# A two-layer attention and MLP stack on one core: start order of the first four tiles, narrow masks, and turns ahead of queries

## The chip, the cores and the metric

The kernel runs on one core of a Trainium2 chip. The metric is device time in microseconds of one execution. The engines are TensorE (PE for matmuls, PEld for its weight loads), VectorE (DVE), ScalarE (ACT), GpSimd (POOL) and SyncE (SP), which issues the DMAs. Each engine runs its own instructions in the order in which they were laid down and waits on semaphores for the others.

## What is computed

Four blocks one after the other on x of shape (1, 2048, 576) in bf16: linear attention A, MLP B, then A and B again with the same weights. Each has a layer norm in front and a residual sum behind.

```python
def _A_ref(x, wqkv, wo):
    B, S, D = x.shape
    H = 32; Dh = D // H
    qkv = (lambda x, *d: x.transpose(*d))((x @ wqkv).reshape(B, S, 3, H, Dh), 2, 0, 3, 1, 4)
    q, k, v = qkv[0], qkv[1], qkv[2]
    phi = lambda t: jnp.where(t > 0, t + 1, jnp.exp(t)) + 1e-6
    pq, pk = phi(q), phi(k)
    kv = jnp.einsum("bhsd,bhse->bhde", pk, v)
    z = jnp.einsum("bhsd->bhd", pk)
    num = jnp.einsum("bhqd,bhde->bhqe", pq, kv)
    den = jnp.einsum("bhqd,bhd->bhq", pq, z)[..., None] + 1e-6
    o = num / den
    return (lambda x, *d: x.transpose(*d))(o, 0, 2, 1, 3).reshape(B, S, D) @ wo

def _B_ref(x, w1, b1, w2, b2):
    y = _layernorm(x, axis=-1)
    h = _gelu(jnp.einsum("bsd,df->bsf", y, w1) + b1)
    return jnp.einsum("bsf,fd->bsd", h, w2) + b2

x = x + _A_ref(_layernorm(x, axis=-1), A_wqkv, A_wo)
x = x + _B_ref(_layernorm(x, axis=-1), B_w1, B_b1, B_w2, B_b2)
x = x + _A_ref(_layernorm(x, axis=-1), A_wqkv, A_wo)
x = x + _B_ref(_layernorm(x, axis=-1), B_w1, B_b1, B_w2, B_b2)
```

## The kernel before

The 2048 rows are 16 tiles of 128. The 576 columns are five blocks of 128 (the last half empty) when they are contracted, and five groups of heads (126, 126, 126, 126 and 72 columns) for the queries. The MLP works on chunks of 512 rows. All matmul operands are bf16; sums are in PSUM, of which four banks form the pool `ps_h` (each holds one product of keys, queries or turned columns until ScalarE or VectorE has read it), and two pairs are accumulators.

The change lies in the first attention layer (`li == 0` in `layer_A`). Its first sweep goes over the tiles t. A tile is loaded from x (`load_x0`), normalised, turned, and then used twice.

*Normalising* is a small pipeline, `LNPipe`. `feed0(t)` puts tile t into it, and each `lnp.tick()` moves every tile one stage on: statistics on VectorE (L363, L364, L370, named s..a, s..b and g.. for the first tiles, and L381, named u..), the reciprocal root (ScalarE's Ln and Exp for tiles 0 and 1, L394 and L396; GpSimd's pow for the others, L399), then the scaling. For tiles 0 to 3 VectorE scales 512 columns (L416, n..) and GpSimd the last 64 into `v_ring` (L414); from tile 4 on GpSimd does both (L402, L410). The last stage is the *turn*: five TensorE transposes into PSUM (`tp`, L464) and copies into `yT` (L466 by ScalarE and L467 by VectorE for tiles 0 to 3, named ca.. and cd..; L469 by ScalarE alone from tile 4 on). A tick with `transposes=0` turns no tile.

*Keys* (`keys(t)`, two `k_half`, L601): ten matmuls of yT with the key weights into two banks. The feature map phi follows in one of two ways: `phi_from_psum` has two ScalarE passes (L511 exp, L512 identity) and two short VectorE instructions on bf16 (L517, L519); `phi_by_dve` has one ScalarE pass (L494) and two VectorE instructions (L496, and L498, which reads the bank). The second half of each tile goes by VectorE, and in tiles 2, 6, 10 and 14 the first half too.

*Queries* (`q_proj(g, c)`, L578): five matmuls for a group of heads g and a chunk c of 512 rows, then phi in the first way. There are twenty; `q_left` holds those still to do, and each takes its place between other work. For g = 0 a memset (L583) writes rows of ones beside the result.

*Sums over rows* (`rows_by_keys(t, half)`, L626): five matmuls of the tile with phi of its keys, added over all tiles. The first sweep does the first half of the columns, a second sweep the second half.

Behind the first sweep the accumulators are copied out (L638, L641), and in the second sweep `kv_groups((0, 1))` (L650) multiplies by the value weights and cuts the heads' blocks out with the mask `maskz` (L656). The denominators use `head_sel` (L742), `quad_mask` (L785) and `head_bc` (L798, L814). These four masks are constants, built on GpSimd by memsets (L70) and affine selects (L66). `masks(n)` issues the next n steps of the list: one per turn for t = 5 to 12, then two per tile in the second sweep; a scheduling edge puts each behind the last normalisation known at that point, and none waits for more.

What sets the order: TensorE's instructions of this layer are chained in program order (`pe`). On VectorE and ScalarE a scheduler places the instructions, and for the first tiles two lists written by hand, `in_order("...")`, fix the sequence by name. In these names e, id, mi and ma are the four steps of phi (L511 or L494, L512, L517 or L496, L519 or L498), followed by tile and half. In a turn t from 4 on the program has keys(t), then `pre_a1(t)` (which feeds tile t + 3, ticks, and issues a piece of weight load on SP), a query, another tick, and the row sums.

Of the kernel before, what the change touches and what calls it, by code (L numbers as in the profile page):

```python
# [8 lines left out]
ALU = mybir.AluOpType  # L9
# [25 lines left out]
def build(tc, A_x, A_wqkv, A_wo, B_w1, B_b1, B_w2, B_b2, out, dbg=None, n_layers=4):  # L35
    nc = tc.nc
    dbg = dbg or {}
    with ExitStack() as ctx:
# [32 lines left out]

        def inner_diag(tile_, lead, n):
            return [fill(tile_, 1.0),
                    select(tile_[:], 0.0, ALU.is_ge, 0, lead(1) + [[-DH, n]] + ([[0, DH]] if tile_ is maskz else []), 1),
                    select(tile_[:], 0.0, ALU.is_ge, DH - 1,
                           lead(-1) + [[DH, n]] + ([[0, DH]] if tile_ is maskz else []), -1)]

        hb = head_bc[:, :, 0:126].rearrange("p g (h d) -> p g h d", h=7)
        mask_steps = inner_diag(maskz, lambda sign: [], 7) + [
            lambda: nc.gpsimd.memset(zsel[96:P, 0, :], 1e-6),  # L80
        ] + inner_diag(head_sel, lambda sign: [[126 * sign, G]], H) + [
            fill(quad_mask, 1.0),
            select(quad_mask[:], 0.0, ALU.is_ge, 0, [[-32, 4], [0, P]], 1),
            select(quad_mask[:], 0.0, ALU.is_ge, 31, [[32, 4], [0, P]], -1),
            fill(head_bc, 0.0),
        ] + [select(hb, 1.0, ALU.not_equal, -32 * quad, [[-7, G], [-1, 7], [0, DH]], 1) for quad in range(4)]

# [225 lines left out]
        class LNPipe:  # L313
# [11 lines left out]
            def tick(self, transposes=1):  # L325
                land()
                for it in list(self.items):
# [77 lines left out]
                    elif st in (2, 3) and it["kind"] == "A" and it["evac"] == "act":  # L405
                        xt, t = it["xt"], it["t"]
                        tail = first_tail(t)[:, 0:64]
                        if it["norm"] == "pool":
                            for out, cols in ((xt[:, 0:4 * P], slice(0, 4 * P)), (tail, slice(4 * P, D))):
                                norm = nc.gpsimd.tensor_scalar(out=out, in0=xt[:, cols], scalar1=it["rstd"][:, 0:1],  # L410
                                                               scalar2=it["nmr"][:, 0:1], op0=ALU.mult, op1=ALU.add)
                            pool_last["norm"] = norm.ins.name
                        else:
                            nc.gpsimd.tensor_scalar(out=tail, in0=xt[:, 4 * P:D], scalar1=it["mv"][:, 0:1],  # L414
                                                    scalar2=it["rstd"][:, 0:1], op0=ALU.subtract, op1=ALU.mult)
                            norm = nc.vector.tensor_scalar(out=xt[:, 0:4 * P], in0=xt[:, 0:4 * P], scalar1=it["mv"][:, 0:1],  # L416
                                                           scalar2=it["rstd"][:, 0:1], op0=ALU.subtract, op1=ALU.mult)
                            dve_last["norm"] = named(f"n{t}", norm).ins.name
                        row_of[t] = xt
# [152 lines left out]
        def layer_A(li, next_kind, pre_a1=None):  # L572
            pq = {}

            def q_proj(g, c, defer=False):
# [6 lines left out]
                if g == 0:  # L582
                    nc.gpsimd.memset(pq[(g, c)][96:P, 0:CA], 1.0)  # L583
                phi = lambda after=None, dve_after=None, exp_first=False: phi_from_psum(qp[0:GR[g], :], pq[(g, c)][0:GR[g], 0:CA], GR[g], CA,
# [13 lines left out]
            def k_half(t, half, defer=False):  # L598
                kp = ps_h.tile([P, 512], F32, name="k_ps", tag="h")
                for k in range(KD):  # L600
                    pe(nc.tensor.matmul(kp[:, 0:HALF], lhsT=yT[:, k, t * P:(t + 1) * P],  # L601
                                        rhs=wqkv_sb[:, k, D + half * HALF: D + (half + 1) * HALF],
                                        start=(k == 0), stop=(k == KD - 1)))
                by_dve = half or li == 0 and t % 4 == 2

# [69 lines left out]
            if li == 0:  # L675
# [4 lines left out]
                def feed_and_tick(t, n):  # L680
                    feed0(t, after=dve_last["phi"] if t > 5 else None)
                    for _ in range(n):
                        lnp.tick()

                k_half(0, 0)
                phi = k_half(0, 1, defer=True)
                keys(1)
                feed_and_tick(3, 2)
                rows_by_keys(0, 0, (0, 1, 2, 3))
                keys(2)  # L690
                phi()
                feed_and_tick(4, 2)
                rows_by_keys(1, 0, (0, 1, 2, 3))
                rows_by_keys(2, 0, (0, 1, 2, 3))
                keys(3)
                q_proj(*q_left.pop(0))
                feed_and_tick(5, 1)
                feed_and_tick(6, 2)
                in_order("s0a s0b s1b g0 s1a g1 n0 n1 cd0 s2a s2b cd1 g2 u2 mi00 s3a ma00 n2 s3b mi10 cd2 g3 mi11 u3 ma11 "
                         "s4b n3 mi20 ma10 ma20 s4a cd3 g4 u4 mi21 mi01 ma21 ma01 s5a s5b mi30 g5 ma30 u5 mi31 ma31")  # L700
                in_order("ln0 re0 ln1 re1 ca0 ca1 e00 id00 e10 e11 ca2 id10 e20 e21 e01 ca3 e30 e31 id30 ca4")
                rows_by_keys(3, 0, (0, 1, 2, 3))
                for t in range(4):
                    rows_by_keys(t, 0, (4,))
                for t in range(4, NT):
                    keys(t)
                    pre_a1(t)
                    if 4 < t < 13:
                        masks(1)
                    q_proj(*q_left.pop(0), defer=True)(after=act_last["turned"])  # L710
                    lnp.tick()
                    rows_by_keys(t, 0)
                for _ in range(2):
                    q_proj(*q_left.pop(0))
            LAG = 3
            steps = [(t, 1) for t in range(NT)] if li == 0 else [(t, half) for half in range(2) for t in range(NT)]
            behind = []
            for n, (t, half) in enumerate(steps):
                if li == 0:
                    masks(2)  # L720
                    rows_by_keys(t, 1)
                    if t == 3:
                        q_proj(*q_left.pop(0))
                else:
# [315 lines left out]
        lnp.tick()  # L1040
        warm_pe(1)
        lnp.tick()

# [77 lines left out]
```

## Time and profile before

| What | Value |
|---|---|
| Runs shown | 767.79, 767.87, 769.43 us; median 767.87 |
| The profiled execution | 769.74 us, of which the span is 767.9 us |
| TensorE matmuls (PE) busy | 757.9 us, 99% of the span, 6538 instructions |
| VectorE, ScalarE, GpSimd busy | 272.5, 326.2 and 129.5 us |
| Chain that ended last | 96% PE, 2% DVE, 1% DMA, 1% ACT |
| Mean granted clock of TensorE | 0.998 |
| First attention layer | 0 to 110 us, the first MLP starts at 110 |

The chain that ended last follows the work back from the end: where it names TensorE, nothing but TensorE's own work stood in the way; where it names another engine, TensorE waited for that engine. A table of waits gives, for each waiting line, the engine and line that ended the wait. The granted clock is the share of TensorE's full speed in a stretch.

By stage, first sweep (columns: stretch in us, its length, then busy time and count of PE, PEld, DVE, ACT, POOL, then clock, share of the DMA engines, GB/s):

```profile
7.60:22.40 14.80, 12.88 (x100) 9.04 (x100) 13.16 (x51) 8.99 (x22) 9.72 (x18) 1.00 1.01 299
29.50:32.80 3.30, 3.30 (x27) 2.38 (x26) 2.77 (x9) 2.73 (x8) 2.32 (x5) 1.00 1.10 287
52.90:59.90 7.00, 4.95 (x26) 3.11 (x25) 4.59 (x8) 2.99 (x7) 5.83 (x8) 0.76 1.00 169
```

### The profile page before, as it was taken

The page shows a single profiled execution, that of the slowest core. Times are in us where ns is not written, and L with a number is a line of the kernel's source. Part 1 is how long each engine was busy: PE and PEld are TensorE (multiplying, and loading weights), DVE is VectorE, ACT ScalarE, POOL GpSimd, SP SyncE. Part 2 cuts the span into 40 slices and gives each one's busy share as a digit, 9 for nine tenths or more (in the row PEclk, how much of TensorE's full clock was granted, in tenths as well). Part 3 has the DMA queues.
Part 4 walks back from the last instruction along what each step waited for, and adds up shares of the span by engine and source line. Part 5 has one row for each costly group of instructions (what it writes and reads, how often), then busy time and mean ns, then how long its engine had stood idle before and what let it go on. Part 6 is the DMA issues. An engine that isn't in the chain of part 4 may idle for free.

```text
span 767.9 us, 15683 instructions
## 1 busy us (share of the span) xinstructions
PE 757.9 (99%) x6538; PEld 489.7 (64%) x6538; DVE 272.5 (35%) x675; ACT 326.2 (42%) x726; POOL 129.5 (17%) x203
## 2 busy tenths in 40 slices
PE   8989999999999999999999999999999999999998
PEld 5667664575477447645777767447745764674476
DVE  8883865035213603400355668610140032000000
ACT  5764766403620560165046568560065027205600
POOL 6781132012100201110110005200020021001000
PEclk9999999999999999999999999999999999999999
DMA  8992373115502631230147007630141033011000
GB/s 254 262 310 48 106 263 99 50 47 144 158 17 64 186 82 40 93 90 1 47 128 233 3 1 220 245 81 13 49 111 52 16 124 82 9 32 55 2 9 24
DMA packets 80897, 73.82 MB, mean 96 GB/s; under 512 B 36730, under 2 KB 65466, under 8 KB 80826
## 3 DMA queue, kind: packets, MB, share of 16 engines
q1 hardware_dynamic: 80826, 72.82, 32.3%
q8 instruction: 51, 0.84, 0.5%
q14 instruction: 20, 0.16, 0.1%
HBM read 48.03 MB, written 24.77 MB: 95 GB/s over the span
## 4 chain that ended last, share of the span: by engine, by line
PE 96%; DVE 2%; DMA 1%; ACT 1%; POOL 0%; issue 0%; SPq 0%; DVEq 0%; POOLq 0%
PE m_ps L1011 36%; PE h_ps L953 20%; PE hp_ps L953 16%; PE q_ps L578 6%; PE wo_ps L834 5%; PE k_ps L601 5%; PE k_ps L626 4%; PE m_half L1011 1%; PE k_tail L626 1%; PE tp L464 1%; DMA wqkv_sb<-in_A_wqkv_dram 1%; PE rden_ps L798 0%; PE kv_ps L650 0%; PE den_ps L771 0%; DVE pq L824 0%
## 5 line engine op out<-in xcount | busy, mean ns | idle before, releaser
L1011 PE MATMUL m_ps<-w_sb,hT 128*128 128x288 bf16 x2232 | 274.8, 286 | 0.0
L1011 PEld LDWEIGHTS <-hT 128*128 128x128 bf16 x2304 | 224.8, 98 | 59.8 <-issue 3.4
L953 PEld LDWEIGHTS <-w_sb 64*128 64x128 bf16 x2304 | 124.5, 94 | 136.4 <-issue 1.9
L953 PE MATMUL hp_ps<-yT,w_sb 64*128 64x512 bf16 x1152 | 178.0, 376 | 0.0
L953 PE MATMUL h_ps<-yT,w_sb 64*128 64x512 bf16 x1152 | 147.9, 376 | 0.0
L958 ACT COPY relay_sb<-relay_sb 128x1 f32<-128x1 f32 x144 | 28.5, 198 | 260.7 <-PE h_ps L953 217.7
L949 ACT ACTIVATE hT<-h_ps,b1T 128x512 bf16<-128x512 f32 x144 | 91.0, 683 | 43.9 <-PE h_ps L953 43.9
L399 POOL TENSOR_TENSOR ln_rstd<-ln_u,neg_half 128x1 f32<-128x1 f32 x62 | 35.9, 581 | 414.1 <-DVE ln_u L381 220.0
L949 ACT ACTIVATE hT<-hp_ps,b1T 128x512 bf16<-128x512 f32 x144 | 91.1, 692 | 0.0
L562 DVE TENSOR_TENSOR xbf<-m_ps,xo 128x576 bf16<-128x576 f32 x15 | 11.4, 758 | 212.3 <-PE m_ps L1011 212.3
L562 DVE TENSOR_TENSOR xo<-m_ps,xo 128x576 f32<-128x576 f32 x16 | 12.1, 758 | 175.6 <-PE m_ps L1011 175.6
L545 POOL TENSOR_TENSOR xo<-xo,b_bc 128x576 f32<-128x576 f32 x32 | 40.9, 1282 | 98.6 <-DMA xo<-x_d 61.0
L953 PE MATMUL h_ps<-yT,w_tail 64*128 64x512 bf16 x144 | 54.1, 376 | 0.0
L953 PE MATMUL hp_ps<-yT,w_tail 64*128 64x512 bf16 x144 | 54.1, 376 | 0.0
L578 PE MATMUL q_ps<-yT,wqkv_sb 128*126 128x512 bf16 (+1 forms) x200 | 50.7, 385 | 2.8 <-DVE pk L498 2.8
L601 PE MATMUL k_ps<-wqkv_sb,yT 128*128 128x288 bf16 x320 | 46.8, 286 | 1.8 <-DVE ln_u L381 0.9
L834 PE MATMUL wo_ps<-kvwo,pq 126*128 126x288 bf16 (+1 forms) x320 | 44.2, 286 | 0.1
L953 PEld LDWEIGHTS <-w_tail 64*128 64x128 bf16 x288 | 27.1, 94 | 17.1
L601 PEld LDWEIGHTS <-yT 128*128 128x128 bf16 x320 | 31.1, 98 | 10.6 <-ACT yT L469 1.2
L834 PEld LDWEIGHTS <-pq 126*128 126x128 bf16 (+1 forms) x320 | 29.8, 97 | 10.0 <-DVE pq L824 0.5
L578 PEld LDWEIGHTS <-wqkv_sb 128*126 128x126 bf16 (+1 forms) x200 | 25.8, 133 | 15.1 <-issue 3.6
L511 ACT ACTIVATE phi_e<-q_ps 126x512 bf16<-126x512 f32 (+1 forms) x40 | 23.9, 598 | 20.2 <-PE q_ps L578 20.2
(132 smaller groups left out, 611.8 us busy)
## 6 DMA issues: line engine op xcount, KB each, us to landing
xo<-x_d SPq DMA_DIRECT2D x48, 288.0 KB
x_d<-xo SPq DMA_DIRECT2D x32, 288.0 KB
xl<-x_d SPq DMA_DIRECT2D x24, 288.0 KB
y_d<-turned SPq DMA_DIRECT2D x40, 144.0 KB
w_sb<-in_B_w_dram SPq DMA_DIRECT2D x6, 864.0 KB
yT<-y_d SPq DMA_DIRECT2D x10, 512.0 KB
w_sb<-in_B_w_dram SPq DMA_DIRECT2D x9, 512.0 KB
x_d<-xn SPq DMA_DIRECT2D x16, 288.0 KB
```

The costliest lines, as they stand in the source:

```text
L399: nc.gpsimd.tensor_tensor(out=rstd[:], in0=it["u"][:], in1=neg_half[:], op=ALU.pow)
L511: exp = nc.scalar.activation(out=e_out, in_=ps_ap, func=ACT.Exp)
L545: nc.gpsimd.tensor_tensor(out=xo[:], in0=xo[:], in1=b2_bc[:], op=ALU.add)
L562: total = nc.vector.tensor_tensor(out=xn[:, cols].rearrange("p (h n) -> p h n", h=2), in0=halves, in1=xo[:, cols].rearrange("p (h n) -> p ...
L578: pe(nc.tensor.matmul(qp[0:GR[g], :], lhsT=wqkv_sb[:, k, GO[g]:GO[g] + GR[g]], rhs=yT[:, k, c * CA:(c + 1) * CA], start=(k == 0), stop=(k ...
L601: pe(nc.tensor.matmul(kp[:, 0:HALF], lhsT=yT[:, k, t * P:(t + 1) * P], rhs=wqkv_sb[:, k, D + half * HALF: D + (half + 1) * HALF], start=(k ...
L626: pe(nc.tensor.matmul(dst, lhsT=lhsT, rhs=pk, start=(t == 0), stop=(t == NT - 1)))
L834: pe(nc.tensor.matmul(wp[:, half, 0:HALF], lhsT=pq[(g, c)][0:GR[g], j * P:(j + 1) * P], rhs=kvwo[g][0:GR[g], half * HALF:(half + 1) * HALF ...
L949: act_last["gelu"] = nc.scalar.activation(out=to, in_=ps, func=ACT.Gelu_apprx_tanh, bias=b1T[:, f:f + 1], scale=1.0).ins.name
L953: mm = pe(nc.tensor.matmul(dst[n], lhsT=wt, rhs=mv, start=(seen[n] == 0), stop=(seen[n] == 8)))
L958: relay = nc.scalar.copy(out=relay_sb[:, 1:2], in_=relay_sb[:, 0:1])
L1011: pe(nc.tensor.matmul(acc[half][:, 0:HALF], lhsT=hT[f][:, j * P:(j + 1) * P], rhs=w2_sb[:, f, half * HALF:(half + 1) * HALF], start=(f == ...
```

## The change

Masks: three of the four masks (`maskz`, `quad_mask`, `head_bc`) are first made narrow on GpSimd, one column per head or quarter in a shared tile `narrow`, and VectorE copies them out to their width in the second sweep (`wide_masks`, t = 0, 1, 2). `head_sel` and a row of `zsel` are made as before. The list now has 15 steps, and `masks(2)` runs in every turn from t = 4.

First tiles: the 64-column tail of tiles 0 to 3 is scaled by VectorE (nt..) instead of GpSimd; the ones rows of the queries are set by VectorE in this layer; only tile 2 has both halves of its keys by VectorE. The keys of tile 0's first half stand ahead of the turn of tile 1, a second warm-up matmul stands in front, two queries are done before t = 4 instead of one, and both `in_order` lists are new. One query less is done in the second sweep (at t = 3).

Turns: in turn 4 a tick stands ahead of the query, and the tick behind the query turns no tile.

```diff
-        def inner_diag(tile_, lead, n):
-            return [fill(tile_, 1.0),
-                    select(tile_[:], 0.0, ALU.is_ge, 0, lead(1) + [[-DH, n]] + ([[0, DH]] if tile_ is maskz else []), 1),
-                    select(tile_[:], 0.0, ALU.is_ge, DH - 1,
-                           lead(-1) + [[DH, n]] + ([[0, DH]] if tile_ is maskz else []), -1)]
-
-        hb = head_bc[:, :, 0:126].rearrange("p g (h d) -> p g h d", h=7)
-        mask_steps = inner_diag(maskz, lambda sign: [], 7) + [
+        narrow = {}
+
+        def narrow_tile():
+            narrow["all"] = blk.tile([P, D], BF16, name="narrow", tag="blk")
+            return nc.gpsimd.memset(narrow["all"][:, 0:64], 1.0)
+
+        def cut(start, shape, fill, op, base, pattern, mult):
+
+            def step():
+                n = shape[0] * shape[-1] if len(shape) > 1 else shape[0]
+                part = narrow["all"][:, start:start + n]
+                if len(shape) > 1:
+                    part = part.rearrange("p (a b) -> p a b", a=shape[0])
+                return nc.gpsimd.affine_select(out=part, in_=part, compare_op=op, fill=fill, base=base, pattern=pattern,
+                                               channel_multiplier=mult)
+            return step
+
+        lead = lambda sign: [[126 * sign, G]]
+        mask_steps = [
+            narrow_tile,
+            cut(0, (7,), 0.0, ALU.is_ge, 0, [[-DH, 7]], 1),
+            cut(0, (7,), 0.0, ALU.is_ge, DH - 1, [[DH, 7]], -1),
+            cut(8, (4,), 0.0, ALU.is_ge, 0, [[-32, 4]], 1),
+            cut(8, (4,), 0.0, ALU.is_ge, 31, [[32, 4]], -1),
+            lambda: nc.gpsimd.memset(narrow["all"][:, 12:47], 0.0),
+        ] + [cut(12, (G, 7), 1.0, ALU.not_equal, -32 * quad, [[-7, G], [-1, 7]], 1) for quad in range(4)] + [
+            fill(head_sel, 1.0),
...
             lambda: nc.gpsimd.memset(zsel[96:P, 0, :], 1e-6),
-        ] + inner_diag(head_sel, lambda sign: [[126 * sign, G]], H) + [
-            fill(quad_mask, 1.0),
-            select(quad_mask[:], 0.0, ALU.is_ge, 0, [[-32, 4], [0, P]], 1),
-            select(quad_mask[:], 0.0, ALU.is_ge, 31, [[32, 4], [0, P]], -1),
-            fill(head_bc, 0.0),
-        ] + [select(hb, 1.0, ALU.not_equal, -32 * quad, [[-7, G], [-1, 7], [0, DH]], 1) for quad in range(4)]
+            lambda: nc.gpsimd.memset(head_bc[:, :, 126:P], 0.0),
+        ]
+
+        def wide_masks(i):
+            small = narrow["all"]
+            if i == 0:
+                wide = nc.vector.tensor_copy(out=maskz[:], in_=small[:, 0:7].unsqueeze(2).to_broadcast([P, 7, DH]))
+            elif i == 1:
+                wide = nc.vector.tensor_copy(out=quad_mask[:], in_=small[:, 8:12].unsqueeze(2).to_broadcast([P, 4, P]))
+            else:
+                wide = nc.vector.tensor_copy(out=head_bc[:, :, 0:126].rearrange("p g (h d) -> p g h d", h=7),
+                                             in_=small[:, 12:47].rearrange("p (g h) -> p g h", g=G).unsqueeze(3)
+                                             .to_broadcast([P, G, 7, DH]))
+            tc.add_manual_dep(wide.ins, dve_last["phi"], NOSYNC, reason="masks are not urgent")
...
-                            nc.gpsimd.tensor_scalar(out=tail, in0=xt[:, 4 * P:D], scalar1=it["mv"][:, 0:1],
-                                                    scalar2=it["rstd"][:, 0:1], op0=ALU.subtract, op1=ALU.mult)
-                            norm = nc.vector.tensor_scalar(out=xt[:, 0:4 * P], in0=xt[:, 0:4 * P], scalar1=it["mv"][:, 0:1],
-                                                           scalar2=it["rstd"][:, 0:1], op0=ALU.subtract, op1=ALU.mult)
-                            dve_last["norm"] = named(f"n{t}", norm).ins.name
+                            for name, out, cols in ((f"n{t}", xt[:, 0:4 * P], slice(0, 4 * P)), (f"nt{t}", tail, slice(4 * P, D))):
+                                norm = named(name, nc.vector.tensor_scalar(
+                                    out=out, in0=xt[:, cols], scalar1=it["mv"][:, 0:1], scalar2=it["rstd"][:, 0:1],
+                                    op0=ALU.subtract, op1=ALU.mult))
+                            dve_last["norm"] = norm.ins.name
...
-                    nc.gpsimd.memset(pq[(g, c)][96:P, 0:CA], 1.0)
+                    (nc.gpsimd if li > 0 else nc.vector).memset(pq[(g, c)][96:P, 0:CA], 1.0)
...
-                by_dve = half or li == 0 and t % 4 == 2
+                by_dve = half or li == 0 and t == 2
...
                 k_half(0, 0)
+                lnp.tick()
                 phi = k_half(0, 1, defer=True)
                 keys(1)
+                phi()
                 feed_and_tick(3, 2)
                 rows_by_keys(0, 0, (0, 1, 2, 3))
                 keys(2)
-                phi()
                 feed_and_tick(4, 2)
                 rows_by_keys(1, 0, (0, 1, 2, 3))
                 rows_by_keys(2, 0, (0, 1, 2, 3))
                 keys(3)
                 q_proj(*q_left.pop(0))
+                phi = q_proj(*q_left.pop(0), defer=True)
                 feed_and_tick(5, 1)
                 feed_and_tick(6, 2)
-                in_order("s0a s0b s1b g0 s1a g1 n0 n1 cd0 s2a s2b cd1 g2 u2 mi00 s3a ma00 n2 s3b mi10 cd2 g3 mi11 u3 ma11 "
-                         "s4b n3 mi20 ma10 ma20 s4a cd3 g4 u4 mi21 mi01 ma21 ma01 s5a s5b mi30 g5 ma30 u5 mi31 ma31")
-                in_order("ln0 re0 ln1 re1 ca0 ca1 e00 id00 e10 e11 ca2 id10 e20 e21 e01 ca3 e30 e31 id30 ca4")
+                phi(after=first_ones["ca4"].ins.name)
+                in_order("s0a s0b g0 s1a s1b n0 nt0 g1 cd0 n1 nt1 s2a s2b g2 cd1 u2 mi00 s3a s3b n2 nt2 g3 ma00 u3 s4a cd2 "
+                         "mi11 mi10 n3 nt3 ma11 ma10 mi20 ma20 cd3 s4b mi01 g4 u4 ma01 s5a s5b mi30 mi21 ma30 g5 ma21 u5 "
+                         "mi31 ma31")
+                in_order("ln0 re0 ln1 re1 ca0 e00 ca1 id00 e10 e11 ca2 e01 id10 e20 e21 ca3 e30 id30 e31 ca4")
                 rows_by_keys(3, 0, (0, 1, 2, 3))
...
                     pre_a1(t)
-                    if 4 < t < 13:
-                        masks(1)
+                    if t == 4:
+                        lnp.tick()
+                    masks(2)
                     q_proj(*q_left.pop(0), defer=True)(after=act_last["turned"])
-                    lnp.tick()
+                    lnp.tick(transposes=0)
                     rows_by_keys(t, 0)
                 for _ in range(2):
                     q_proj(*q_left.pop(0))
+                masks(len(mask_steps))
...
                 if li == 0:
-                    masks(2)
+                    if t in (0, 1, 2):
+                        wide_masks(t)
                     rows_by_keys(t, 1)
-                    if t == 3:
-                        q_proj(*q_left.pop(0))
...
-        warm_pe(1)
-        lnp.tick()
+        warm_pe(2)
```

## The prediction

> **What bounds the kernel now.** The page comes first: TensorE is busy 99% of the span of 767.9 us and has 96% of the chain that ended last, so time is won only where TensorE stands still or runs slowly, or where the chain leaves it. The page's clock row shows only nines, because one of its slices covers 19.2 us. I therefore read TensorE's waits over the first 110 us, which contain the whole first attention layer:
>
> ```profile
> PE q_ps L578 <- DVE pk L498: 2.8, 3, 2.1
> PE warm_ps L185 <- DVE y_ring L180: 1.3, 1, 1.3
> PE k_ps L601 <- DVE ln_u L381: 0.9, 1, 0.9
> PE k_ps L601 <- DMA wqkv_sb<-in_A_wqkv_dram: 0.5, 1, 0.5
> PE tp L464 <- POOL x L410: 0.4, 1, 0.4
> PE k_ps L601 <- ACT phi_a L512: 0.4, 1, 0.4
> ```
>
> The columns after the colon are total us, times, longest. Everything idle is in the stage that the diff touches, and 2.1 us of it is one wait. The chain of waits around it:
>
> ```profile
> 51.13 1.16 PE q_ps L578 x5
> 52.30 0.02 issue
> 52.32 0.60 ACT phi_e L511
> 52.92 0.02 issue
> 52.95 1.29 DVE phi_e L517
> ...
> 54.35 0.63 DVE pq L519
> 54.98 0.94 DVE phi_e L496
> 55.92 0.02 issue
> 55.94 0.47 DVE pk L498
> 56.41 0.04 issue
> 56.45 2.29 PE q_ps L578 x5
> 58.74 0.24 PE k_tail L626
> 58.98 0.96 PE k_ps L626 x4
> 59.94 1.26 PE k_ps L601 x10
> ```
>
> The chain leaves TensorE for ScalarE and VectorE, and when it comes back the same five query matmuls take 2.29 us instead of 1.16. The timeline shows who held VectorE, and the table by stage shows why the matmuls were slow (columns: us, then busy time and count of PE, PEld, DVE, ACT, POOL, then granted clock, DMA share, GB/s):
>
> ```profile
> 54.66 4.27 POOL L66 TENSOR_SCALAR_AFFINE_SELECT head_bc<-head_bc 128x630 bf16<-128x630 bf16 x4
> 54.91 1.00 DVE L496 TENSOR_SCALAR phi_e<-phi_e 128x288 bf16<-128x288 bf16 x1
> ```
>
> ```profile
> 55.00:56.00 1.00, 0.00 (x0) 0.00 (x0) 0.96 (x2) 0.15 (x1) 0.93 (x2) 1.00 1.16 279
> 57.00:58.00 1.00, 1.00 (x4) 0.51 (x3) 0.44 (x1) 0.00 (x0) 0.93 (x2) 0.50 1.38 21
> ```
>
> The L496 form takes 0.23 us in quiet tiles and 1.00 here. The wide selects of 1.016 us start at 54.66, so the second ends near 56.7 and the first near 55.67; L496 ends at 55.91, which is 55.67 plus its usual 0.23. VectorE's bf16 tensor_scalar waited out a whole GpSimd instruction. After 2.05 us without a matmul the clock was 0.50 until about 59.5.
>
> **The hole (masks).** Key tiles in quiet turns start 3.27 us apart (L601 at 29.42, 32.69, 35.95, 39.22). From 52.73 to 59.74 it took 7.01, and the next ten key matmuls 1.47 instead of 1.39. The hole is worth 3.74 + 0.08 = 3.82 us, of which 2.05 is idle and some 1.77 the half clock. The change removes its cause: the wide GpSimd steps are 0.21 + 2 x 0.334 (maskz), 0.52 + 2 x 0.664 (quad_mask), 0.64 + 4 x 1.016 (head_bc), 7.43 us. In their place stand ten narrow steps (7 to 64 columns). No row has such a form; the bounds are 0.10 (memset 128x1) and 0.35 us (select 128x160), and I take 0.20, near the 0.21 of the 36-column copy L222, so 2.0 us in all, two to four steps per turn. GpSimd works some 2.3 us of each 3.3 us turn, and a turned tile is ready 1.1 us ahead (x and tail of tile 14 end at 49.60, its turn starts at 50.69), which hides them. Uncovered, 0.7 us per turn would show. The steps end by t = 11, long before the masks' first use (kv_ps, 70.4). Gain 3.82, with 2.05 as the low end if the clock fell for another reason.
>
> **Spreading.** Three VectorE copies of 126 + 512 + 630 elements. Bounds: 0.65 us at the pace of tensor_scalar (512 in 0.24 to 0.29), 1.67 at that of the f32 sums (576 in 0.758); they read with a repeat, so I take 1.67. They stand behind the last query's phi and ahead of kvT. VectorE has 5.2 of 10 us free between 60 and 70, and in the new order it is through some 1.5 us ahead of the kv_ps product. Cost 0; uncovered 1.67 at most.
>
> **Keys of tiles 6, 10, 14.** Before, both halves of these tiles went over VectorE's L496/L498, which free the PSUM bank late: the turns from 25.70 to 29.42 and 39.22 to 42.94 took 3.72 us instead of 3.27. Only tile 2 keeps this. ScalarE gets one pass more (L512, 0.31 to the next start), exactly what it does in the quiet turns, where it still waits 0.43 us for each query. Gain 2 x 0.45 = 0.90; the third lies in the hole.
>
> **Ones rows of the queries.** Four memsets of 32x512 move from GpSimd (0.56 each, one of which held tile 4's normalisation from 15.23 to 15.75) to VectorE. By the row of 128x320 in 0.33 us it is 0.53, bounds 0.33 and 0.78 (64x864). VectorE has some 0.3 us free per turn (2.94 us from one L363 to the next in the turn at 32.26, of 3.27), and a product of keys is ready 0.6 to 0.75 us before TensorE wants it; I cost it at 0, uncovered 3 x 0.53 in the loop.
>
> **The start.** I went through the new order by hand with the durations above, keeping the DMA times. Tile 0 is ready 0.24 us earlier because s1 no longer stands ahead of g0, and its 64-column tail comes from VectorE (bounds 0.15, ln_u, and 0.41, 128x512; I take 0.17) instead of GpSimd (0.71). None of it counts: the second half of the key weights lands at 7.63, as before. From there: keys of tiles 0 and 1 until 9.7; tile 2's copies end at 10.83, so its keys start at 10.87 (before 10.88); tile 3 is turned at 12.2 instead of 12.29, keys 3 start at 13.84 instead of 13.77, because product 2 waits for ma20 behind the later e20. The first query is at 15.1, and now the second follows at once at 16.25, while GpSimd finishes tile 4 at 16.75 (before 17.09: u4 is 0.3 later, the memset of 0.53 is gone). TensorE is at tile 4's turn at 17.4, not held; the 0.44 is gone. Keys 4 at 18.66, tile 5's turn at 19.9 (ready at 19.35), its copy done at 21.1 behind the third query, keys 5 at 21.97 without the 0.87. Before it was 22.42, with one query less. That query is taken out of the later loop, where it cost 1.08 (67.50). From t = 5 on the old order already had the turn ahead of the query, so nothing more comes from that. Gain 0.45 + 1.08 = 1.53. Bounds: if all VectorE additions (4 x 0.17 + 0.53 = 1.2) fall on the path, 0.3; if the 0.41 before keys 2 also closes, 1.95.
>
> **Sum.** 3.82 + 0.90 + 1.53 = 6.25 us. The profiled execution is 769.74 us for a span of 767.9, so 1.84 lie around the span; with the change 763.5 in the same measure. The median of the runs is 767.87, 1.87 below that execution, and I carry the difference over: 761.6. The later stages move forward as they are: SP's order is unchanged, the weight loads end near 60 us either way, and w_sb is first needed at 110.
>
> **Rivals.**
> 1. VectorE bounds the start: it has 13.2 of 14.8 us busy between 7.6 and 22.4, and gets five instructions more, 1.2 us. Against: it stands still for 1.6 us there, and my pass found place for them. Start gain 0.3, so 767.87 - 5.02 = 762.9.
> 2. The clock did not fall because of the gap, and the 1.77 stays: 763.4. For it speaks only that the other gaps, up to 0.87 us, left the clock at 1.00, so no row gives a threshold; against it, that it fell at the end of the longest gap. The Trainium skill ("TensorE: Matmul & The Clock Gate", What's actually happening) puts the fall after an idle window of about 3.4 us. By that rule a gap of 2.05 us would not do, and the sum would be 4.5; the trace (0.50 right behind 2.05 us) speaks otherwise.
> 3. The stall moves: GpSimd's extra steps make each tile late at its turn, which now stands ahead of the query at every t. At 0.3 us in 11 turns, 3.3 us: 764.9. Against: the 1.1 us in hand.
> 4. Slower: the half clock comes at the start. In the new hand-written order s4a, which needs tile 4's row from DRAM, stands near 9.95 and ahead of tile 2's copy; before, it stood at 12.92. If the row landed only then (the latest that the trace allows, as s4a did not wait), the keys of tile 2 would wait some 2.3 us, longer than the 2.05 that halved the clock before. Each us of TensorE work done at 0.50 costs one us more, so it decides against the change from 6.25 us of such work less the wait itself, some 4; if all 12.9 us of work between 7.6 and 22.4 ran so, the time would be 767.87 - 6.25 + 12.9 = 774.5. Against: the gap at 54.4 cost only 1.77 in this way, and summed over half microseconds the DMA rates put tile 4's row at about 8.5.
> 5. All of it cancels within 0.2%: some 767.9.
>
> **How the numbers follow.** Forecast 0.62; rival 1 0.13, rival 2 0.06, rival 3 0.09, rival 4 0.06, rival 5 0.04. The predicted time is the forecast's. About 0.2% (1.5 us) is what a measurement of this kernel can tell from no change. Faster: 0.62 + 0.13 + 0.06 + 0.09 = 0.90; same 0.04; slower 0.06. The range's low end takes the better start and 0.5 us for small waits in the two loops, 760.7; its high end takes rival 3 and the bound of the ones rows at one place, 765.4. Above lie rivals 4 and 5, below little.
>
> **What would show it.** Turns of 3.27 us from t = 5 to 15 with clock 1.00 throughout, no wait of q_ps for pk L498, no GpSimd instruction above 0.85 us between 22 and 60, keys 5 near 22.0, and the second sweep starting near 59.8 instead of 64.9. Wrong would be a granted clock below 1 after 6 us, waits of tp for GpSimd's x, DVE copies of the masks ending after kv_ps, or k_ps waiting for copies between 10 and 14 us by more than 0.4.

## The result and the profile after

| What | Before | After |
|---|---|---|
| Median of the runs measured together | 768.21 us (4 runs, 767.79 to 769.43) | 763.48 us (4 runs, 763.10 to 763.75) |
| Ratio, 95% interval | | 0.9935 [0.9918, 0.9953] |
| A second measurement on another occasion | 768.27 us (15 runs) | 763.32 us (5 runs), 0.9932 [0.9918, 0.9945] |
| The profiled execution, its span | 769.74, 767.9 us | 763.75, 762.0 us |
| GpSimd busy | 129.5 us | 119.9 us |

The change makes the kernel faster by some 4.8 us. The forecast was 761.6 us within 760.7 to 765.4; the time lies inside, 1.9 us above the forecast. Profiled execution against profiled execution the step is 5.9 us of span where 6.25 were forecast, so the 1.9 is not a gain that failed to come: it is mostly a matter of what was compared with what, as the runs below show.

TensorE's waits over the first 110 us after the change (engine, line and tile that waited, the engine and line waited for, then total us, times, longest):

```profile
PE warm_ps L214 <- DVE y_ring L209: 1.3, 1, 1.3
PE k_ps L630 <- DVE yT L496: 0.4, 1, 0.4
PE k_ps L655 <- DVE pk L527: 0.3, 1, 0.3
```

The three waits of queries for VectorE's pk (2.8 us), the 0.9 before keys 5, the 0.5 for the key weights' DMA, the 0.4 for GpSimd's x and the 0.4 for phi_a are gone; what is left sits ahead of 14 us. The three stretches shown for the kernel before, or their counterparts (stretch, length, busy time and count of PE, PEld, DVE, ACT, POOL, then clock, DMA share, GB/s):

```profile
52.90:59.90 7.00, 7.00 (x47) 4.86 (x45) 4.58 (x15) 5.76 (x15) 0.00 (x0) 1.00 1.02 178
22.20:57.80 35.60, 35.60 (x272) 26.58 (x270) 29.90 (x104) 28.99 (x66) 23.26 (x53) 1.00 1.01 286
7.60:22.40 14.80, 14.09 (x113) 10.16 (x112) 13.41 (x52) 10.02 (x25) 7.15 (x14) 1.00 1.01 296
```

Between 52.90 and 59.90 GpSimd does nothing now, TensorE is busy for all 7.00 us (4.95 before) and the clock is 1.00 (0.76 before). In the whole first sweep from tile 5 on TensorE has no gap. VectorE's share of the start rose by only 0.25 us (13.16 to 13.41), GpSimd's fell by 2.57.

What the new instructions cost, from the groups of GpSimd over the first 64 us (count, busy us, mean ns) and from VectorE's timeline (start, duration):

```profile
L85 POOL TENSOR_SCALAR_AFFINE_SELECT narrow<-narrow 128x35 bf16<-128x35 bf16 x4 | 1.1, 284 | 0.1
L85 POOL TENSOR_SCALAR_AFFINE_SELECT narrow<-narrow 128x4 bf16<-128x4 bf16 x2 | 0.5, 264 | 0.0
L76 POOL MEMSET narrow<- 128x64 bf16 x1 | 0.2, 153 | 0.0
```

```profile
62.20 0.28 DVE L108 CAST maskz<-narrow 128x126 f32<-128x126 bf16 x1
62.40 0.42 DVE L110 COPY quad_mask<-narrow 128x512 bf16<-128x512 bf16 x1
62.73 0.80 DVE L112 COPY head_bc<-narrow 128x630 bf16<-128x630 bf16 x1
65.04 0.42 DVE L685 TENSOR_TENSOR kvT<-kv_ps,maskz 126x252 bf16<-126x252 f32 x1 [1.51 <-PE kv_ps L679]
```

The narrow steps are 4 to 64 columns wide (the prediction said 7 to 64) and take 0.12 to 0.28 us where 0.20 was put down, 2.3 us in all instead of 2.0. The three spreading copies take 1.50 us together (1.67 was put down), and VectorE then stands still for 1.51 us until TensorE's kv_ps: they are hidden.

### The profile page after: what moved, and what is told of

It reads as the page before. It is cut to its first block, busy times and chain, and to the rows that moved or that the text cites. A ratio compares the mean times of both kernels' runs of the same rounds, so it can differ in the third digit from the quotient of the medians.

```text
span 762.0 us, 15698 instructions
## 1 busy us (share of the span) xinstructions
PE 756.5 (99%) x6539; PEld 489.6 (64%) x6539; DVE 271.0 (36%) x686; ACT 326.6 (43%) x729; POOL 119.9 (16%) x195
## 4 chain that ended last, share of the span: by engine, by line
PE 97%; DVE 2%; ACT 0%; issue 0%; ACTq 0%; DVEq 0%
PE m_ps L1045 36%; PE h_ps L987 20%; PE hp_ps L987 16%; PE q_ps L607 6%; PE k_ps L630 5%; PE wo_ps L868 4%; PE k_ps L655 4%; PE m_half L1045 1%; PE k_tail L655 1%; PE tp L493 1%; PE warm_ps L214 1%; PE rden_ps L832 0%; PE kv_ps L679 0%; DVE xn L591 0%; DVE pq L858 0%
## 5 line engine op out<-in xcount | busy, mean ns | idle before, releaser
L1045 PEld LDWEIGHTS <-hT 128*128 128x128 bf16 x2304 | 224.8, 98 | 59.8 <-issue 3.4
L540 ACT ACTIVATE phi_e<-k_ps 128x288 bf16<-128x288 f32 x31 | 12.8, 412 | 41.5 <-PE k_ps L630 39.3
```

What stands on the lines that cost most here:

```text
L540: exp = nc.scalar.activation(out=e_out, in_=ps_ap, func=ACT.Exp)
L1045: pe(nc.tensor.matmul(acc[half][:, 0:HALF], lhsT=hT[f][:, j * P:(j + 1) * P], rhs=w2_sb[:, f, half * HALF:(half + 1) * HALF], start=(f == ...
```

## The experiments

The edits below are against the kernel before or the changed one, as each says. Starts of keys in TensorE's timeline (us) are the common scale, because from tile 5 on a quiet turn takes 3.27 us everywhere:

| Kernel | keys 5 | keys 14 | keys 15 | span | median of runs |
|---|---|---|---|---|---|
| before, first profile | 22.42 | 52.73 | 59.74 | 767.9 | 768.21 |
| before, e5 | 22.10 | 52.40 | 59.43 | 767.5 | 769.37 (one) |
| before, e6 | 22.24 | 52.54 | 57.96 | 766.0 | 767.91 (one) |
| e1 masks alone | 22.44 | 52.99 | 56.71 | 764.6 | 766.55 |
| e2 keys alone | 22.38 | 51.76 | 56.70 | 764.6 | 766.51 |
| e3 start alone | 21.81 | 52.50 | 56.50 | 764.0 | 766.00 |
| e7 masks and keys | 22.48 | 51.88 | 55.14 | 763.1 | 764.91 |
| e4 changed, old masks | 22.20 | 51.63 | 54.90 | 764.7 | 764.71 |
| after, first profile | 22.20 | 51.64 | 54.90 | 762.0 | 763.48 |
| after, e11 | 21.91 | 51.35 | 54.61 | 761.6 | 763.32 |
| e12 start reordered | 22.79 | 52.23 | 55.49 | 762.4 | 764.28 |

### One part alone: e1, e2, e3

e1 takes the new list of masks, `wide_masks` and the two calls of `masks`, and leaves the rest of the kernel before:

```diff
-                    if 4 < t < 13:
-                        masks(1)
+                    masks(2)
...
-                    masks(2)
+                    if t in (0, 1, 2):
+                        wide_masks(t)
                     rows_by_keys(t, 1)
```

> The kernel before with only the masks made narrow on GpSimd and spread by VectorE. Theory (wide selects hold VectorE, the gap halves the clock): the hole of 3.82 us closes, but tile 14's keys still go over VectorE alone, 0.45, so 3.37 us less, about 764.5 us by the median before of 767.9; granted clock 1.00 from 52 to 60 us. Rival (the half clock has another cause than the gap): only the idle part goes, 1.6 us less, 766.3, and the clock still falls near 56 us. Rival (the spreading copies are not hidden): 1.5 us of the gain come back between 60 and 70 us, 766.0.

Measured: 766.55 us, 0.9974 [0.9964, 0.9985]. The clock is 1.00 throughout and no wide select holds VectorE any more. Tile 14's turn takes 3.72 us, exactly the 0.45 too long that its keys cost. From the first profile to this one the span fell by 3.3 us (767.9 to 764.6), as the theory had it. Yet the median fell by only 1.3 us against the 767.9 of the expectation, and by 2.1 against the 768.62 measured beside it. The spreading was not to blame, since no wait stands between 60 and 72 us. Tile 10's turn took 3.97 instead of 3.72. The trace shows where VectorE fell behind, one turn earlier:

```profile
37.34 0.42 DVE L548 TENSOR_TENSOR pq<-phi_a,phi_e 126x512 bf16<-126x512 bf16 x1 [0.79 <-POOL pq L612]
```

It waits 0.79 us for GpSimd's memset of the ones rows (0.43 before), because `masks(2)` now puts a select of `head_sel` (0.36 us) ahead of that memset, and VectorE's steps behind it start 0.38 later. In the changed kernel VectorE sets these rows itself, so it does not wait for GpSimd there.

e2 shares the first-half keys of tiles 6, 10 and 14 between ScalarE and VectorE, and leaves the wide masks:

```diff
-                by_dve = half or li == 0 and t % 4 == 2
+                by_dve = half or li == 0 and t == 2
```

> The kernel before with only the first-half keys of tiles 6, 10 and 14 given to both ScalarE and VectorE. Theory: the turns of tiles 6 and 10 take 3.27 instead of 3.72 us, tile 14's 0.45 lies in the hole that stays, so 0.9 us less, 767.0. Rival (ScalarE's extra pass delays the queries by as much): nothing, 767.9. Rival (the hole is set by tile 14's late bank, not by the selects): about 4.2 us less, 763.7.

Measured: 766.51 us, 0.9970 [0.9959, 0.9980]. The two turns are 3.27 as expected, so the 0.9 is there; but the hole shrank as well. TensorE's timeline of this run (start, duration, in brackets the wait ahead of it and who ended it), and the clock in the same place:

```profile
53.34 1.24 PE L578 MATMUL q_ps<-yT,wqkv_sb 128*126 128x512 bf16 x5
56.09 0.28 PE L626 MATMUL k_tail<-pk,v_ring 128*65 128x288 bf16 x1 [1.51 <-DVE pk L519]
```

```profile
55.00:56.00 1.00, 0.00 (x0) 0.00 (x0) 0.95 (x2) 0.70 (x2) 0.93 (x2) 1.00 1.31 166
56.00:57.00 1.00, 0.91 (x8) 0.73 (x8) 0.97 (x4) 0.00 (x0) 1.00 (x1) 1.00 1.53 27
```

The wide selects are all there, VectorE is held as before, but the gap is 1.51 us instead of 2.05 and the clock behind it is 1.00. In seven runs (766.19 to 766.73) none lies 1.5 us above the others, and the mean granted clock of each is 1.000. Tile 14's keys had a share in the hole: in the kernel before the query itself waited for pk L498 behind a held L496; here it starts at once (53.34), and only the row sums wait. Tile 14's turn is 4.94 us.

e3 takes only the new beginning (an excerpt; the new orders are those of the whole change):

```diff
-                            nc.gpsimd.tensor_scalar(out=tail, in0=xt[:, 4 * P:D], scalar1=it["mv"][:, 0:1],
...
+                            for name, out, cols in ((f"n{t}", xt[:, 0:4 * P], slice(0, 4 * P)), (f"nt{t}", tail, slice(4 * P, D))):
...
-                    nc.gpsimd.memset(pq[(g, c)][96:P, 0:CA], 1.0)
+                    (nc.gpsimd if li > 0 else nc.vector).memset(pq[(g, c)][96:P, 0:CA], 1.0)
...
+                phi = q_proj(*q_left.pop(0), defer=True)
...
-                    lnp.tick()
+                    lnp.tick(transposes=0)
```

> The kernel before with only the new beginning: orders, tails and ones rows on VectorE, two queries ahead of tile 4, the turns ahead of the queries. Theory, from the changed kernel's profile (its first sweep runs 0.25 us later than the 1.53 forecast): 1.3 us less, 766.6, with keys of tile 5 near 22.2 us. Rival (the beginning brings nothing by itself, and what was won elsewhere is larger than forecast): 767.9. If the early matmuls at half pace (7.68 us end of tile 0's first keys, where the kernel before had 7.17) come from the new order and not from chance, this run shows them too, and the next one; the two runs ahead, with the old beginning, do not.

Measured: 766.00 us, 0.9968 [0.9956, 0.9981]. Keys 5 start at 21.81, better than forecast; and again the hole is smaller, 0.64 us ahead of tile 14's query and 0.50 in the next turn, with the clock at 1.00.

So each part alone brings 2.1 to 2.6 us by the medians (768.62 before, measured beside them; together 6.8), all three 4.7 to 5.0. They share something, and all three lack one thing that the first profile of before has: the half clock.

### The hole's second half: e5, e6

Looking again at the kernel before, its 48 runs over all occasions spread from 767.51 to 770.37 us. For 44 of them the mean granted clock of the whole run is on record. In 28 runs, between 767.51 and 769.05 us, it is 0.999 or 1.000; in 16, between 769.26 and 770.37, it is 0.997 or 0.998. The profiled execution of 769.74 (0.998) belongs to the 16. No run of any changed version has less than 0.999. A high time alone does not show the half clock, though: single runs of other versions (769.64 in e8, 766.44 in e4) lie more than 1 us above their fellows at 1.000. What spreads the 28 over 1.5 us was not followed. So the unchanged kernel was profiled twice more.

> The kernel before, unchanged, for another profiled execution. Its times so far fall into two groups, 767.5 to 767.9 and 768.4 to 769.7 us. Theory: the groups are one hole with and without the half clock behind it. An execution near 767.6 shows the same gap of about 2.05 us at the query of tile 14 and a granted clock of 1.00 after it, and tile 15's keys start near 58.0; one near 769.5 shows 0.5 and 59.7. Rival: the groups differ elsewhere, and the half clock is there each time.

> The same once more, since which group an execution falls into looks like chance; the same two theories and numbers.

Measured: 769.37 and 767.91 us, one of each. TensorE's timeline of e5 and its stretch from 57 to 58 us, then the same two of e6:

```profile
56.14 2.29 PE L578 MATMUL q_ps<-yT,wqkv_sb 128*126 128x512 bf16 x5 [2.07 <-DVE pk L498]
58.23 0.44 PE L626 MATMUL k_tail<-pk,v_ring 128*65 128x288 bf16 x1
58.47 1.16 PE L626 MATMUL k_ps<-pk,x 128*128 128x288 bf16 x4
```

```profile
57.00:58.00 1.00, 1.00 (x4) 0.58 (x3) 0.13 (x1) 0.00 (x0) 0.93 (x2) 0.50 1.47 55
```

```profile
56.27 1.24 PE L578 MATMUL q_ps<-yT,wqkv_sb 128*126 128x512 bf16 x5 [2.07 <-DVE pk L498]
57.35 0.29 PE L626 MATMUL k_tail<-pk,v_ring 128*65 128x288 bf16 x1
57.47 0.65 PE L626 MATMUL k_ps<-pk,x 128*128 128x288 bf16 x4
```

```profile
57.00:58.00 1.00, 1.00 (x9) 0.69 (x8) 0.27 (x1) 0.45 (x1) 0.93 (x2) 1.00 0.82 9
```

The same program, the same gap of 2.07 us, and behind it the query takes 2.29 us in one execution and 1.24 in the other, the granted clock being 0.50 and 1.00. Tile 14's turn takes 7.03 and 5.42 us; with 0.06 in the next keys the half clock costs 1.67. The theory holds, its number for keys 15 too (58.0 expected, 57.96 measured). Worked out from the clock of stretches of 0.1 and 0.2 us, it stood at 0.50 from 56.48 to 59.89 in the first profile and from 56.13 to 59.56 in e5, 3.4 us each time (the prediction read the end as about 59.5). Half of 3.4 is the 1.7 us that the half clock costs.

### Two parts together: e7, e4

> The kernel before with the narrow masks and the shared keys, with the old beginning. Theory: with no hole left, tiles 6, 10 and 14 each give back 0.45 us against the masks alone: 766.55 - 1.35 = 765.2 us, all turns 3.27 us from tile 5, clock 1.00; the new beginning is then worth 765.2 - 763.5 = 1.7. Rival (masks and keys close the same hole, so that together they bring no more than one of them): 766.5.

Measured: 764.91 us, 0.9948 [0.9933, 0.9962], every turn from tile 5 to 15 at 3.26 to 3.28 us. Without a hole masks and keys add up: 1.64 less than the masks alone, of which 0.25 is the longer turn of tile 10 in e1. The new beginning is worth 764.91 - 763.32 = 1.6 by the medians.

e4 is the changed kernel with the old list of masks, `masks(1)` for t = 5 to 12 and `masks(2)` in the second sweep.

> The changed kernel with only the old wide masks put back, steps where they stood before. Theory: the hole comes back with its gap and its half clock, 3.4 to 3.9 us more than the changed kernel's 763.5, so 766.9 to 767.4, granted clock near 0.5 behind the gap. Rival (with the keys of tile 14 shared and the turns ahead of the queries the selects no longer reach the path): 763.5 to 764.0. Rival (the gap comes back, but the clock holds): 765.3 to 765.6.

Measured: 764.71 us, 0.9949 [0.9934, 0.9963], some 1.3 more than the changed kernel; neither 3.4 to 3.9 nor nothing. (Its profiled execution took 766.44, the other runs 764.53 to 765.04. Beyond the hole it waited 0.6 us once for a residual sum, in the second attention layer, which no other profile here shows; the rest of its distance was not followed.) The gap now falls into tile 15's turn. GpSimd's selects and VectorE's timeline, then TensorE's:

```profile
53.86 4.20 POOL L66 TENSOR_SCALAR_AFFINE_SELECT head_bc<-head_bc 128x630 bf16<-128x630 bf16 x4
53.99 1.00 DVE L496 TENSOR_SCALAR phi_e<-phi_e 128x288 bf16<-128x288 bf16 x1
55.02 0.46 DVE L498 SCALAR_TENSOR_TENSOR pk<-k_ps,phi_e 128x288 bf16<-128x288 f32 x1
55.39 0.69 DVE L517 TENSOR_SCALAR phi_e<-phi_e 126x512 bf16<-126x512 bf16 x1
56.19 1.03 DVE L519 TENSOR_TENSOR pq<-phi_a,phi_e 126x512 bf16<-126x512 bf16 x1
57.15 0.99 DVE L517 TENSOR_SCALAR phi_e<-phi_e 128x288 bf16<-128x288 bf16 x1
```

```profile
58.61 0.28 PE L626 MATMUL k_tail<-pk,v_ring 128*65 128x288 bf16 x1 [1.23 <-DVE pk L519]
```

Three of VectorE's five instructions last about 1.0 us, as one select does (1.05), where they take 0.22 to 0.43 in quiet turns; the query's L517, which starts in the middle of a select, lasts 0.69 instead of 0.28. It is not only tensor_scalar that is held, as the prediction had it: the bf16 tensor_tensor of two tiles in SBUF is held too (1.03). L498, which reads PSUM, keeps its 0.46. The Trainium skill ("SBUF — State Buffer", SBUF: two separate sides) says that GpSimd and VectorE's operations in a two-port mode or with two SBUF inputs take a shared pair of ports in turn, for a whole instruction; the trace agrees for these five instructions. With turns and keys in the new form the selects cost 1.23 us of gap, and the clock holds.

### How long a gap it takes: e8, e9, e10

> The changed kernel with 3, 4 and 5 more VectorE copies of 128x630 (0.80 us each, into the block mask that is overwritten later) ahead of the keys of tiles 6, 9 and 12, which hold TensorE up for some 1.7, 2.5 and 3.3 us. Theory (the clock is judged over stretches that do not begin with the gap, so that chance decides between some 1.5 and 3.4 us): 1.00 behind the shortest, 0.5 behind the longest, either behind the middle one; times spread over some 2 us or more, 771 to 775. Rival (only a gap of about 3.4 us or more counts, by the Trainium skill, TensorE: Matmul & The Clock Gate, What's actually happening): 1.00 behind all three, 771.0, little spread. Rival (any gap over 1.5 us counts): 0.5 behind all three, about 776.

Measured: 768.30 us, ten runs between 768.14 and 768.54 but for one of 769.64. The scheduler spread the copies between the steps of phi, so TensorE stood still in pieces of at most 1.15 us, and the clock was 1.00 behind each. The run says nothing about longer gaps.

e9 and e10 try to make TensorE wait for the copies' result; `stall(n)` lays down n copies and a small product (`hold_ps`) that reads what they wrote:

```diff
+                    if t in {6: 1, 8: 2, 10: 3, 12: 4}:
+                        stall({6: 1, 8: 2, 10: 3, 12: 4}[t])
                     masks(2)
                     q_proj(*q_left.pop(0), defer=True)(after=act_last["turned"])
```

> The changed kernel with one more small product in the turns of tiles 6, 8, 10 and 12, ahead of the query, that reads the result of 1, 2, 3 and 4 VectorE copies of 128x630 (0.80 us each, into the block mask that is overwritten later): TensorE stands in one piece for some 1.3, 2.1, 2.9 and 3.7 us. The run with three gaps never held it longer than 1.15 us and so told nothing of the limit. Theory (chance between some 1.5 and 3.4 us, surer the longer the gap): 1.00 behind the first, sometimes 0.5 behind the second, mostly 0.5 behind the third, always behind the fourth; the times scatter by 1.7 us or its double. Rival (a fixed limit near 2.05 us, met or missed by a few hundredths): 0.5 behind the second to fourth every time, or from the third on every time, and times within 0.5 us of one another. Rival (only from about 3.4 us on, by the Trainium skill, TensorE: Matmul & The Clock Gate, What's actually happening): 0.5 behind the fourth alone.

> The same kernel once more, for a second profiled execution: by the theory of chance the second or third gap may come out the other way than in the first; by both rivals with a fixed limit none does.

Measured: 767.57 us (ten runs, 767.52 to 768.16) and 767.59. This did not give the longer gaps either. TensorE's timeline of e9 at the fourth place:

```profile
48.30 0.28 PE L663 MATMUL k_tail<-pk,v_ring 128*65 128x288 bf16 x1 [1.05 <-DVE pk L556]
...
50.48 0.19 PE L123 MATMUL hold_ps<-head_bc 128*126 128x64 bf16 x1
```

The product that was to wait found its copies done: the scheduler had put them earlier, where they delayed pk instead, and the longest gap was 1.05 us. What stays from both kernels is that a program with several gaps of up to 1.15 us was granted 1.00 behind each of them, and repeats to within 0.1 us in most runs. From which gap on the clock can fall is left open between 1.51 us (never seen) and 2.05 (seen in some executions). A fixed limit alone does not fit e5 and e6, where the same gap of 2.07 us ends both ways.

### The start: e11, e12

> The changed kernel unchanged, for a second profile and a closer time. Theory: the clock at the beginning rises at another moment in each execution (by the matmuls' durations at 5.2 us in two executions so far, at 6.3, 6.9 and 7.4 in others), so the keys of tile 5 start anywhere from 21.8 to 22.2 us; 763.1 to 763.8 us. Rival: the late rise belongs to this kernel, 22.2 again.

Measured: 763.32 us (763.23 to 763.44), 0.9932 [0.9918, 0.9945]; keys 5 at 21.91. TensorE's timeline in the first profile of the changed kernel, then in e11, then in e3, where the same matmuls stand in the same order:

```profile
5.72 1.06 PE L214 MATMUL warm_ps<-y_ring 128*128 128x512 bf16 x2
6.58 1.10 PE L630 MATMUL k_ps<-wqkv_sb,yT 128*128 128x288 bf16 x5
```

```profile
5.72 0.96 PE L214 MATMUL warm_ps<-y_ring 128*128 128x512 bf16 x2
6.51 0.78 PE L630 MATMUL k_ps<-wqkv_sb,yT 128*128 128x288 bf16 x5
```

```profile
5.61 0.59 PE L185 MATMUL warm_ps<-y_ring 128*128 128x512 bf16 x2
6.50 0.79 PE L601 MATMUL k_ps<-wqkv_sb,yT 128*128 128x288 bf16 x5 [0.30 <-ACT yT L466]
```

The granted-clock column says 1.00 in all three, so it does not show this; the durations do. Five key matmuls take 0.78 us at full pace and 1.10 in the execution where the pace rose only within them. The late rise also appears with the old beginning (e1, whose turn of tile 0 takes 0.61 us instead of 0.40, and e6, the unchanged kernel, with the same 0.61), so it belongs to the execution and not to the change.

e12 tries to close the two small waits that remain:

```diff
-                        if first and t < 2:
+                        if first and t < 3:
...
-                         "mi11 mi10 n3 nt3 ma11 ma10 mi20 ma20 cd3 s4b mi01 g4 u4 ma01 s5a s5b mi30 mi21 ma30 g5 ma21 u5 "
+                         "mi11 ma11 mi10 n3 nt3 ma10 mi20 ma20 cd3 s4b mi01 g4 u4 ma01 s5a s5b mi30 mi21 ma30 g5 ma21 u5 "
```

> The changed kernel with tile 2's turn written into two PSUM banks, as tiles 0 and 1 have it, so that VectorE's copy (cd2) need not follow ScalarE's, and with VectorE's product ma11 ahead of tile 3's normalisation, so that the exponentials of tile 2 need not wait for its buffer. Theory: the 0.41 us ahead of tile 2's keys shrink by 0.3 and the 0.29 ahead of tile 2's rows go, 0.3 to 0.6 us less than the changed kernel beside it, about 763.0. Rival (ScalarE is the next in line there and takes the place of both): no difference.

Measured: 764.28 us, 0.9947 [0.9934, 0.9959], 1.0 slower than the changed kernel beside it. Two of TensorE's waits in it:

```profile
PE tp L493 <- ACT yT L495: 0.7, 1, 0.7
PE k_ps L630 <- DVE pk L527: 0.5, 1, 0.5
```

The waits of 0.20 to 0.41 us ahead of tile 2's keys and of 0.29 ahead of its rows are gone, but the second bank for tile 2's turn is a bank of the same four, and it was not free: the fourth transposition waited 0.70 us for a copy by ScalarE. Another 0.45 stands ahead of keys 4, and 0.2 at a turn that waits for GpSimd. Which of the two edits brings which wait was not separated. No version faster than the changed kernel was found.

## Why the prediction was right, and where it was not

**The sum.** 6.25 us were forecast against a profiled execution of the kernel before; 5.9 (767.9 to 762.0) and 6.3 (to 761.6, e11) came. Against an execution of before without the half clock (e6, 766.0) it is 4.4, and the starts of keys give its parts: 0.33 until keys 5, 0.86 between keys 5 and 14, 2.16 in tile 14's turn, 1.08 for the query taken out of the second sweep, 4.43 together. That the measured 763.48 lies within the range all the same is luck: its high end of 765.4 was set by a GpSimd late at the turns (rival 3), which did not come, and by the ones rows, which cost some 0.07.

**The step that failed** is the one that "carried the difference over": 769.74 of the profiled execution stand 1.87 above the median of the runs, and the forecast subtracted both the 1.87 and a sum that contained 1.77 of half clock. They are the same microseconds. The profiled execution had the half clock; the two lower runs shown, by their times of 767.79 and 767.87, did not; and the changed kernel's nine runs (763.10 to 763.75) all have a mean clock of 0.999 or 1.000. 769.74 - 6.25 = 763.49 is the time in the right measure, and 763.48 and 763.32 were measured. The time of 763.4 stood there as rival 2. Its cause, a clock that fell for another reason and stays low afterwards, did not come; but its arithmetic, no half clock in the gain, is what the median asks for.

**The hole (3.82).** Closed, with clock 1.00. Its parts were mis-sized. The half clock (1.67 in e5 against e6, 1.77 forecast) comes in some executions and not in others with the same gap, in 16 of 44 runs of the kernel before; the prediction took it as the sure consequence of the gap. The idle part is not the masks' alone: of the 2.15 us by which tile 14's turn in e6 (5.42) exceeds a quiet one, e1 closes 1.70 by the masks, e2 closes 0.48 by tile 14's keys with the selects still there, and e3 closes 1.42 by the beginning and the turns, with 0.50 of it back in the next turn. And in a kernel with new keys and turns the old masks cost only 1.3 (e4).

**Keys (0.90).** Right: the turns of tiles 6 and 10 take 3.26 to 3.27 in e2, e7 and after; the third share in the hole was 0.48.

**Spreading and ones rows (0).** Right: 1.50 us of copies end 1.51 ahead of need; a memset of 32x512 takes 0.48 us on VectorE (0.53 forecast), with no listed wait behind it from tile 5 on. Tile 7's turn, which holds one of them, takes 3.33 us after the change (3.34 in e11) and 3.27 in e7, where GpSimd sets the rows: some 0.07, nearly nothing.

**The start (1.53).** Between the profiles 0.22 + 1.08 = 1.30, and 0.33 + 1.08 = 1.41 for e6 against e11; e3, where full pace comes early, has 0.29 to 0.61 + 1.08 against the three profiles of before. The first of these also waited 0.52 us for the key weights, which e5 and e6 did not, so its keys 5 (22.42) were a late mark to count from. The tails cost 0.30 each rather than 0.17, and the clock's late rise moved keys 5 by 0.3 to 0.4 between executions. Keys 2 were forecast at 10.87 and came at 11.14 in the late execution and 10.86 in e11; the second sweep starts at 59.98 in the late one (59.8 forecast).

**Rivals.** VectorE as the bound of the start (1): no, the start gained 1.30 to 1.41 us and not 0.3, and 0.7 us of waits for VectorE are left there. GpSimd late at the turns (3): no wait of tp for x. Half clock through an early s4a (4): its wait did not occur, keys 2 waited 0.20 to 0.41 us, at the edge of the 0.4 that the prediction named as a sign of being wrong. Of its signs of being right, two GpSimd instructions of 0.87 and 0.88 us lie just above the 0.85 named; both are normalisations of x, not selects.

## What to carry to other kernels

Before taking a profile as the baseline, see where its own time lies among the runs: a gain read from one execution must be set against that execution, or else against the median with everything that only some executions have taken out first. Parts of a change that close the same gap don't add: each alone already took TensorE's gap below the 2.05 us at which the half clock was seen, so by the medians ablations one at a time sum to 6.8 us for a change worth 4.7 to 5.0. Counted in spans from e6, which has no half clock, they sum to 4.8 (1.4, 1.4 and 2.0) for 4.0 to 4.4, so most of the excess is the half clock, counted three times. Long elementwise work on GpSimd is worth making narrow: here VectorE's bf16 instructions between SBUF tiles waited out whole selects of about 1.05 us, although GpSimd was busy for only 17% of the span of the kernel before.

## What the hardware showed

The same gap of 2.07 us in the same program brought a granted clock of 0.50 in one execution and 1.00 in another; over all runs of the kernel before, 16 of 44 have the lower mean clock. The half clock lasted 3.4 us in both profiles that show it. A gap of 1.51 us, measured in one profile of a kernel, left all seven of its runs at 1.000. At the beginning the matmuls reached full pace at about 5.2 us in some executions (before, e3) and only inside the keys that start at 6.58 in another, though the warm-up began at 1.31 or 1.32 us in each. The Trainium skill ("TensorE: Matmul & The Clock Gate", What's actually happening) explains the second with an activity window that runs freely and does not start with the kernel, shifting the change by about 500 ns; the traces agree that the moment varies while the warm-up starts alike, with a scatter nearer 2 us, but no run here shows the window itself. It lets the clock fall after an idle window of about 3.4 us; here it fell behind 2.05 and 2.07 us without a matmul, which that rule does not give.
